# A linear-attention kernel feeding a two-layer perceptron: an earlier slot plan, half of the first q as float32, kv in two banks, and 12 idle matmuls ahead of the first turn of x

## The chip, the cores and the metric

The kernel runs on one core of one Trainium2 chip. The metric is the device time of one execution in microseconds (us). Before the change three runs gave 328.69, 330.32 and 331.72 us; the median is 330.32 us. TensorE (PE) does the matrix products and some transposes, VectorE (DVE) and ScalarE (ACT) the elementwise work, GpSimd (POOL) issues the loads that convert float32 to bfloat16, SyncE (SP) issues the stores and the transposing DMAs.

## The reference

Eight batches, eight heads, 576 positions, head size 64; model width 512, hidden width 2048.

```
kv  = einsum('bhsd,bhse->bhde', k, v)
out = einsum('bhsd,bhde->bhse', q, kv)
rms = sqrt(mean(out * out, axis=-1, keepdims=True) + 1e-06)
x   = (out / rms * g_norm)            # then laid out as (batch, position, 512)

mu, var = mean and variance of x over the 512
xn  = (x - mu) / sqrt(var + 1e-06) * g_ln
y   = x + maximum(xn @ w_ch1, 0.0) @ w_ch2
```

Inputs and the output are float32.

## The kernel before

**Tiling.** The 576 positions of a batch are spread over 128 partitions and four or five places each: partitions 0 to 63 hold five positions, partitions 64 to 127 hold four. A batch so has four full tiles of 128 positions and a remainder of 64; the remainders of two batches are put together into one tile ("rem", four of them).

**The steps of a batch b.** `load_batch` issues six DMAs on POOL (two each for k, v, q; they convert to bfloat16; `k_in`, `v_in`, `q_in` have two buffers, used by even and odd batches). `kv_of` does 40 small matmuls (L162) into one PSUM tile and copies the two diagonal halves into `kv_pack` (DVE L166, ACT L167). q has to be transposed: for batches 0 to 2 by PE (`q_turns`: DVE reorders q into `q_p`, L326; PE transposes, L140; ACT copies, L144), for the later ones by a transposing DMA (`turn_q_dma`: POOL reorders, L151; SP issues the DMA, L153). Per tile, `main_tile` does four matmuls (L179) and a chain (`tile_chain`): ACT square L182, DVE sum `ss` L184, ACT root L186, DVE reciprocal `inv` L188, then DVE `y` L190, `x_blk` L191, `stats` L193, their aggregate L194 and `xc` L196. `turn_x` transposes `xc`: on PE (L206, with an ACT copy L207) for batches 0 to 2, by a transposing DMA on SP (L209) for the others. `mm1` is the first layer (PE L268, ACT relu L271), `mm2` the second (PE L300, DVE sum `o_sb` L304, stores on SP).

**The order.** PE's order is written out by hand: it executes its instructions in the order in which the program issues them. The perceptron's matmuls are cut into slots, and `tick()` starts each slot: a slot of `mm2` is 4 matmuls of 512 columns, a slot of `mm1` is 4 of 512, 8 of 256 or 16 of 128. Batch 0 has slots 0 to 15 (first layer) and 16 to 31 (second), batch 1 has 32 to 47 and 48 to 63, batch 2 starts at 64, batch 3 at 96, and so on, 32 slots each; the remainder block is the last. An agenda says ahead of which slot kv, the turn of q, each tile and each turn of x of a later batch are put into PE's stream (`at`, the table `PLAN` and its defaults). The other engines are in-order as well, but their order is made by a planner from priorities (`due`); `keep_in_program_order` fixes the place of one instruction.

**Where the slots lie in the profile.** The first matmul of slot 0 starts at 27.05 us, that of slot 16 at 44.63, of slot 32 at 75.69; slot 64 begins with a tile at 120.49, slot 112 with a kv at 166.67. Ahead of slot 0 lie the start's loads, `q_turns(0)`, `kv_of(0)`, two tiles, and the turn of x of the first.

**Buffers that the text speaks of.** `qt_pool` holds three transposed q; one is given back when the remainder tile of its batch has been done. `ps_out` has two PSUM buffers, shared by the q transposes and the tiles. `outp` has four output tiles.

Of the kernel before, what the change touches and what calls it, by code (L numbers as in the profile page):

```python
# [2 lines left out]

# [11 lines left out]
def kernel(  # L15
# [11 lines left out]
    nc = tc.nc  # L27
# [51 lines left out]
    v_in = [consts.tile([128, H, JJ, D], bf16, name=f"v_in{i}") for i in range(NB)]  # L79
    kv_pack = [consts.tile([128, HP, 128], bf16, name=f"kv_pack{i}") for i in range(4)]  # L80

    def load(dst, t, b, h0=0, h1=H):
        nc.gpsimd.dma_start(dst[:64, h0:h1],
                            t[b, h0:h1, :S_LO, :].rearrange("h (p j) d -> p h j d", j=JJ))
        nc.gpsimd.dma_start(dst[64:, h0:h1, :J],  # L85
                            t[b, h0:h1, S_LO:, :].rearrange("h (p j) d -> p h j d", j=J))


    load(q_in[0], q, 0)
    nc.vector.memset(eps_sb, float(EPS))  # L90
    nc.scalar.activation(warm, eps_sb, func=AF.Sqrt)
    for i in range(NB):
# [50 lines left out]
                identity[:n, :n])  # L143
        nc.scalar.copy(q_t[:, j, :, :n], tp[:, :, :n])  # L144

    qts, held, blks, xcs = {}, {}, {}, {}

    def turn_q_dma(b):

        q_p = kv_in.tile([128, JJ, H, D], bf16, tag="qp", bufs=2)  # L150
        nc.gpsimd.tensor_copy(q_p.rearrange("p j h d -> p h j d"), q_in[b % NB])  # L151
        q_t = qt_pool.tile([128, JJ, HP, 128], bf16, tag="qt")
        nc.sync.dma_start_transpose(  # L153
            q_t.rearrange("p j hp t -> p (j hp) t"), q_p.rearrange("p j h d -> p (j h d)"))
        qts[b] = q_t

    def kv_of(b):
        kv_ps = ps_m.tile([128, HP, D], f32, tag="misc")
        for h in range(H):
            rows = slice(h % 2 * D, h % 2 * D + D)  # L160
            for j in range(JJ):
                nc.tensor.matmul(kv_ps[rows, h // 2, :], lhsT=k_in[b % NB][:, h, j, :],  # L162
                                 rhs=v_in[b % NB][:, h, j, :],
                                 start=(j == 0), stop=(j == JJ - 1))
        kvp = kv_pack[b % 4]
        nc.vector.tensor_copy(kvp[:D, :, :D], kv_ps[:D])  # L166
        nc.scalar.copy(kvp[D:, :, D:], kv_ps[D:])  # L167
        held[b] = kvp

    def tile_chain(mms, blk, ts, key):  # L170

        x_blk, mv_blk, xT_blk = blk
        x3 = x_blk[:, ts].rearrange("p (h d) -> p h d", h=H)
        x2 = x_blk[:, ts]
        o_ps = ps_out.tile([128, H, D], f32, tag="ops")
        o_flat = o_ps.rearrange("p h e -> p (h e)")
        for (rows, lhsT_of, kvp) in mms:
            for hp in range(HP):
                nc.tensor.matmul(o_flat[rows, hp * 128:(hp + 1) * 128],  # L179
                                 lhsT=lhsT_of(hp), rhs=kvp[:, hp, :], start=True, stop=True)  # L180
# [7 lines left out]
        nc.vector.reciprocal(inv, rms)  # L188
        y = work.tile([128, H, D], f32, tag="y")
        nc.vector.tensor_mul(y, o_ps, inv.to_broadcast([128, H, D]))  # L190
# [5 lines left out]
        nc.vector.scalar_tensor_tensor(xc, in0=x2, scalar=mv_blk[:, ts, 0:1], in1=g_ln_sb,  # L196
                                       op0=ALU.subtract, op1=ALU.mult)
        xcs[key] = xc

    def turn_x(blk, ts, key, on_pe):  # L200
        xc = xcs.pop(key)
# [120 lines left out]

    def q_turns(b):
        q_p = kv_in.tile([128, JJ, H, D], bf16, tag="qp", bufs=2)
        tc.keep_in_program_order(
            nc.vector.tensor_copy(q_p.rearrange("p j h d -> p h j d"), q_in[b % NB]))  # L326
# [8 lines left out]
    for j in (0, 1):  # L335
        due(-90 + 10 * j)
        main_tile(0, j)
    due(-90)
    turn_x(blks[0], 0, (0, 0), True)
    due(-70)  # L340
    main_tile(0, 2)


    PLAN = {1: dict(kv=23, q=23, tiles=[24, 26, 28, 30], turns=[32, 36, 40, 40], rem=48), 3: dict(load=28)}
    S1 = {1: 32, 2: 64}
    for b in range(1, B):
        p = PLAN.get(b, {})
# [66 lines left out]
```

## Time and profile before

| what | value |
|---|---|
| median of three runs | 330.32 us (328.69 to 331.72) |
| the profiled execution's own time | 331.43 us |
| its span, first to last instruction | 329.7 us |
| mean granted TensorE clock | 0.971 |
| PE busy | 283.2 us (86% of the span) |
| DVE busy | 172.5 us (52%) |
| ACT busy | 134.8 us (41%) |
| POOL busy | 52.8 us (16%) |
| last matmul of the run ends | 325.06 us |

The profile is of one execution. Busy time is the time in which an engine has at least one instruction running. Matmuls overlap each other, so PE can be busy all the time at quite different rates. "Granted clock" (PEclk) is the share of full TensorE clock that the chip's throttle gave. Idle time is written in square brackets behind an instruction, with what ended it.

### The profile page before, as it was taken

The page shows a single profiled execution, that of the slowest core. Times are in us where ns is not written, and L with a number is a line of the kernel's source. Part 1 is how long each engine was busy: PE and PEld are TensorE (multiplying, and loading weights), DVE is VectorE, ACT ScalarE, POOL GpSimd, SP SyncE. Part 2 cuts the span into 40 slices and gives each one's busy share as a digit, 9 for nine tenths or more (in the row PEclk, how much of TensorE's full clock was granted, in tenths as well). Part 3 has the DMA queues.
Part 4 walks back from the last instruction along what each step waited for, and adds up shares of the span by engine and source line. Part 5 has one row for each costly group of instructions (what it writes and reads, how often), then busy time and mean ns, then how long its engine had stood idle before and what let it go on. Part 6 is the DMA issues. An engine that isn't in the chain of part 4 may idle for free.

```text
span 329.7 us, 5123 instructions
## 1 busy us (share of the span) xinstructions
PE 283.2 (86%) x2032; PEld 154.3 (47%) x2060; DVE 172.5 (52%) x322; ACT 134.8 (41%) x265; POOL 52.8 (16%) x69
## 2 busy tenths in 40 slices
PE   0328997598792899997999999999999999999994
PEld 0318964347671444543444444445444444444441
DVE  3167403859764898199728745981884260010011
ACT  1325733246671237423731761274257116305500
POOL 7533405071421410302030000000000000000000
PEclk9999998969997899999999999999999999999998
DMA  7999999969829972499368401830331131031022
GB/s 100 199 206 203 201 201 174 200 89 223 109 48 169 167 132 51 65 203 166 80 91 150 97 18 37 171 65 18 80 80 34 32 87 25 2 84 43 2 64 64
DMA packets 61687, 34.84 MB, mean 106 GB/s; under 512 B 28256, under 2 KB 56928, under 8 KB 61664
## 3 DMA queue, kind: packets, MB, share of 16 engines
q0 software_dynamic: 29600, 18.35, 39.5%
q1 hardware_dynamic: 32064, 16.16, 24.0%
q8 instruction: 16, 0.26, 0.3%
q14 instruction: 7, 0.06, 0.1%
HBM read 37.00 MB, written 9.44 MB: 141 GB/s over the span
## 4 chain that ended last, share of the span: by engine, by line
PE 74%; DVE 10%; DMA 6%; ACT 4%; issue 3%; POOL 1%; POOLq 0%; DVEq 0%; SPq 0%; ACTq 0%
PE p L268 35%; PE p L300 34%; DMA v_in<-in_v_dram 3%; DMA q_t<-q_p 3%; DVE xc L196 2%; PE o_ps L179 2%; PE kv_ps L162 2%; DVE x_blk L191 1%; DVE ss L184 1%; DVE y L190 1%; DVE o_sb L304 1%; ACT xT_blk L207 1%; DVE stats L193 1%; ACT qt L144 1%; ACT m L271 1%
## 5 line engine op out<-in xcount | busy, mean ns | idle before, releaser
L268 PE MATMUL p<-xT_blk,w_sb 128*128 128x512 bf16 (+2 forms) x887 | 130.7, 306 | 4.6 <-ACT xT_blk L207 2.3
L300 PE MATMUL p<-w_sb,m 128*128 128x512 bf16 x557 | 131.8, 388 | 1.6 <-issue 0.8
L271 ACT ACTIVATE m<-p 128x512 bf16<-128x512 f32 x144 | 84.1, 594 | 43.9 <-PE p L268 42.9
L268 PEld LDWEIGHTS <-w_sb 128*128 128x128 bf16 x896 | 73.4, 100 | 56.2 <-issue 5.2
L300 PEld LDWEIGHTS <-m 128*128 128x128 bf16 x576 | 55.9, 100 | 64.3 <-issue 3.9
L304 DVE SCALAR_TENSOR_TENSOR o_sb<-p,rstd,x_blk 128x512 f32<-128x512 f32 x36 | 26.9, 746 | 91.6 <-PE p L300 79.6
L182 ACT ACTIVATE sq<-o_ps 128x512 f32<-128x512 f32 x36 | 21.4, 596 | 61.4 <-PE o_ps L179 61.1
L184 DVE TENSOR_REDUCE ss<-sq 128x8 f32<-128x512 f32 x36 | 24.3, 679 | 17.1 <-ACT sq L182 17.1
L196 DVE SCALAR_TENSOR_TENSOR xc<-x_blk,mv_blk,g_ln_sb 128x512 bf16<-128x512 f32 x36 | 32.8, 911 | 0.9
L190 DVE TENSOR_TENSOR y<-o_ps,inv 128x512 f32<-128x512 f32 x36 | 24.8, 690 | 3.2 <-PE o_ps L179 0.5
L193 DVE BATCH_NORM_STATS2 stats<-x_blk 128x6 f32<-128x512 f32 x36 | 24.9, 690 | 0.8
L191 DVE TENSOR_TENSOR x_blk<-y,g_norm_sb 128x512 f32<-128x512 f32 x36 | 24.7, 687 | 0.8
L140 PE MATMUL tp<-identity,q_p 128*128 128x128 bf16 (+1 forms) x60 | 6.7, 268 | 18.0 <-DVE q_p L326 16.4
L186 ACT ACTIVATE rms<-ss,eps_sb 128x8 f32<-128x8 f32 x36 | 10.8, 301 | 24.9 <-DVE ss L184 24.5
L151 POOL COPY q_p<-q_in 128x2560 bf16<-128x2560 bf16 x5 | 11.6, 2325 | 36.1 <-DMA q_t<-q_p 22.5
L85 POOL DMA_DIRECT2D k_in<-in_k_dram x8 | 6.0, 753 | 56.0 <-PE kv_ps L162 55.7
L166 DVE CAST kv_pack<-kv_ps 64x256 bf16<-64x256 f32 x8 | 3.3, 411 | 21.5 <-PE kv_ps L162 21.4
L140 PEld LDWEIGHTS <-q_p 128*128 128x128 bf16 (+1 forms) x60 | 5.1, 123 | 19.7 <-DVE q_p L326 17.0
L179 PE MATMUL o_ps<-kv_pack,q_t 128*128 128x128 bf16 (+1 forms) x100 | 9.2, 224 | 5.9 <-DMA q_t<-q_p 5.8
L206 PE MATMUL tp<-identity,xc 128*128 128x128 bf16 x48 | 5.1, 234 | 9.4 <-DVE xc L196 7.8
L144 ACT COPY qt<-tp 128x512 bf16<-128x512 bf16 (+1 forms) x15 | 7.5, 545 | 13.6 <-PE tp L140 13.6
L179 PEld LDWEIGHTS <-q_t 128*128 128x128 bf16 (+1 forms) x100 | 7.0, 101 | 11.6 <-DMA q_t<-q_p 6.3
(32 smaller groups left out, 101.6 us busy)
## 6 DMA issues: line engine op xcount, KB each, us to landing
out_dram<-o_sb SPq DMA_DIRECT2D x72, 128.0 KB, 2.3
w_sb<-in_moe_w_ch_dram POOLq DMA_DIRECT2D x8, 512.0 KB, 13.3
q_in<-in_q_dram POOLq DMA_DIRECT2D x8, 320.0 KB, 9.4
k_in<-in_k_dram POOLq DMA_DIRECT2D x8, 320.0 KB, 7.9
v_in<-in_v_dram POOLq DMA_DIRECT2D x7, 320.0 KB, 7.9
q_in<-in_q_dram POOLq DMA_DIRECT2D x8, 256.0 KB, 8.9
k_in<-in_k_dram POOLq DMA_DIRECT2D x8, 256.0 KB, 6.8
v_in<-in_v_dram POOLq DMA_DIRECT2D x7, 256.0 KB, 9.5
```

Source lines behind the costliest of these rows:

```text
L140: nc.tensor.transpose(tp[:, hp, :n], q_p[:n, j, 2 * hp:2 * hp + 2, :].rearrange("p h d -> p (h d)"), identity[:n, :n])
L179: nc.tensor.matmul(o_flat[rows, hp * 128:(hp + 1) * 128], lhsT=lhsT_of(hp), rhs=kvp[:, hp, :], start=True, stop=True)
L182: nc.scalar.activation(sq, o_ps, func=AF.Square)
L184: nc.vector.tensor_reduce(ss, sq, axis=AX.X, op=ALU.add)
L190: nc.vector.tensor_mul(y, o_ps, inv.to_broadcast([128, H, D]))
L191: nc.vector.tensor_mul(x3, y, g_norm_sb.to_broadcast([128, H, D]))
L193: nc.vector.bn_stats(stats, x2)
L196: nc.vector.scalar_tensor_tensor(xc, in0=x2, scalar=mv_blk[:, ts, 0:1], in1=g_ln_sb, op0=ALU.subtract, op1=ALU.mult)
L268: nc.tensor.matmul(p1[:, i, :], lhsT=w1_sb[:, kk, de * 128:(de + 1) * 128], rhs=blk[2][:, kk, sl], start=(kk == 0), stop=(kk == nK - 1))
L271: nc.scalar.activation(m1[:, de0:de0 + per, sl], p1, func=AF.Relu)
L300: nc.tensor.matmul(p2s[ts], lhsT=m1[:, de, ts * 128:(ts + 1) * 128], rhs=w2_sb[:, de, :], start=(de == 0), stop=(de == nDe - 1))
L304: nc.vector.scalar_tensor_tensor(o_sb, in0=p2s[ts], scalar=rstds.pop((b, ts))[:, ts], in1=blks[b][0][:, ts], op0=ALU.mult, op1=ALU.add)
```

## The change

- The upper half of the first q (partitions 64 to 127) is loaded as float32 by SP, ahead of the two small constants, into a buffer of `m1pool`; DVE converts it in `q_turns(0)`. The lower half is still loaded by POOL. POOL so issues seven loads ahead of the first weights instead of eight.
- `kv_of(0)` writes odd and even heads into two PSUM banks and works in two parts (four heads each); each part is copied into `kv_pack` when it is done.
- For batch 0, the part of a tile's chain from `y` on (now `tile_x`) is queued on DVE behind the `xc` of the tile before.
- 12 matmuls of 512 columns, whose result nobody reads, are put into PE's stream after the first two tiles and ahead of the first turn of x.
- The DMA turn of q (batches 3 to 7) reorders q on DVE in program order instead of on POOL; `qt_pool` has four buffers.
- The plan: batch 1's kv goes from slot 23 to 13, its q from 23 to 16, its tiles from 24, 26, 28, 30 to 17, 20, 24, 29, its turns of x from 32, 36, 40, 40 to 26, 31, 37, 40; the first remainder tile from 48 to 58. Batch 2's kv goes from 26 to 40, q from 27 to 41, tiles from 32, 38, 44, 50 to 42, 46, 51, 55, turns from 41, 47, 53, 59 to 51, 56, 60, 63. Batch 3: load from 28 to 17, kv from 48 to 56, q from 36 to 54, tiles from 52, 58, 64, 70 to 62, 67, 72, 77. The load of batch 4 goes from 40 to 42, of batch 5 from 72 to 58.
- The first layer of batch 1 takes its first two tiles together (256 columns instead of 128).

```
-    qt_pool = ctx.enter_context(tc.tile_pool(name="qt_pool", bufs=3))
+    qt_pool = ctx.enter_context(tc.tile_pool(name="qt_pool", bufs=4))
...
+    q_f = m1pool.tile([128, H, J, D], f32, tag="m1")
...
-    load(q_in[0], q, 0)
+    nc.sync.dma_start(q_f[64:], q[0, :, S_LO:, :].rearrange("h (p j) d -> p h j d", j=J))
+    nc.gpsimd.dma_start(q_in[0][:64], q[0, :, :S_LO, :].rearrange("h (p j) d -> p h j d", j=JJ))
...
     def turn_q_dma(b):
         q_p = kv_in.tile([128, JJ, H, D], bf16, tag="qp", bufs=2)
-        nc.gpsimd.tensor_copy(q_p.rearrange("p j h d -> p h j d"), q_in[b % NB])
+        tc.keep_in_program_order(
+            nc.vector.tensor_copy(q_p.rearrange("p j h d -> p h j d"), q_in[b % NB]))
...
     def kv_of(b):
         kv_ps = ps_m.tile([128, HP, D], f32, tag="misc")
-        for h in range(H):
-            rows = slice(h % 2 * D, h % 2 * D + D)
-            for j in range(JJ):
-                nc.tensor.matmul(kv_ps[rows, h // 2, :], lhsT=k_in[b % NB][:, h, j, :],
-                                 rhs=v_in[b % NB][:, h, j, :],
-                                 start=(j == 0), stop=(j == JJ - 1))
+        odd = ps2.tile([128, HP, D], f32, tag="p2", name="odd") if b == 0 else kv_ps
         kvp = kv_pack[b % 4]
-        nc.vector.tensor_copy(kvp[:D, :, :D], kv_ps[:D])
-        nc.scalar.copy(kvp[D:, :, D:], kv_ps[D:])
+        n = 2 if b == 0 else 1
+        for part in range(n):
+            for h in range(part * H // n, (part + 1) * H // n):
+                rows = slice(h % 2 * D, h % 2 * D + D)
+                for j in range(JJ):
+                    nc.tensor.matmul((odd if h % 2 else kv_ps)[rows, h // 2, :],
+                                     lhsT=k_in[b % NB][:, h, j, :], rhs=v_in[b % NB][:, h, j, :],
+                                     start=(j == 0), stop=(j == JJ - 1))
+            hps = slice(part * HP // n, (part + 1) * HP // n)
+            nc.vector.tensor_copy(kvp[:D, hps, :D], kv_ps[:D, hps])
+            nc.scalar.copy(kvp[D:, hps, D:], odd[D:, hps])
         held[b] = kvp
...
         nc.vector.reciprocal(inv, rms)
+        after = last_xc.get(chain) if chain is not None else None
+        with tc.issue_after(after) if after is not None else nullcontext():
+            last = tile_x(o_ps, inv, x_blk, mv_blk, ts, key)
+        if chain is not None:
+            last_xc[chain] = last.ins
...
-        tile_chain([(slice(0, 128), lambda hp: q_t[:, j, hp, :], kvp)], blks[b], j, (b, j))
+        tile_chain([(slice(0, 128), lambda hp: q_t[:, j, hp, :], kvp)], blks[b], j, (b, j),
+                   0 if b in (0,) else None)
...
     def q_turns(b):
         q_p = kv_in.tile([128, JJ, H, D], bf16, tag="qp", bufs=2)
-        tc.keep_in_program_order(
-            nc.vector.tensor_copy(q_p.rearrange("p j h d -> p h j d"), q_in[b % NB]))
+        if b == 0:
+            nc.vector.tensor_copy(q_p[64:, :J].rearrange("p j h d -> p h j d"), q_f[64:])
+            nc.vector.tensor_copy(q_p[:64].rearrange("p j h d -> p h j d"), q_in[0][:64])
+        else:
+            tc.keep_in_program_order(
+                nc.vector.tensor_copy(q_p.rearrange("p j h d -> p h j d"), q_in[b % NB]))
...
     for j in (0, 1):
         due(-90 + 10 * j)
         main_tile(0, j)
+
+    for n in (12,):
+        p1 = ps1.tile([128, 512], f32, tag="p1", name="p1")
+        for i in range(n):
+            nc.tensor.matmul(p1, lhsT=identity, rhs=qts[0][:, 0].rearrange("p a b -> p (a b)"),
+                             start=True, stop=True)
+        del p1
     due(-90)
     turn_x(blks[0], 0, (0, 0), True)
...
-    PLAN = {1: dict(kv=23, q=23, tiles=[24, 26, 28, 30], turns=[32, 36, 40, 40], rem=48), 3: dict(load=28)}
+    PLAN = {1: dict(kv=13, q=16, tiles=[17, 20, 24, 29], turns=[26, 31, 37, 40], rem=58),
+            2: dict(kv=40, q=41, tiles=[42, 46, 51, 55], turns=[51, 56, 60, 63]),
+            3: dict(load=17, kv=56, q=54, tiles=[62, 67, 72, 77]), 4: dict(load=42), 5: dict(load=58)}
...
-    mm1(1, 0, 1)
-    mm1(1, 1, 1)
+    mm1(1, 0, 2)
     mm1(1, 2, 2)
```

More of the change, by code (lines that the diff above doesn't have):

```diff
@@ L2 @@
 import logging
-from contextlib import ExitStack
+from contextlib import ExitStack, nullcontext
 import concourse.bass as bass
@@ L158, in kv_of, with tile_chain @@
         kv_ps = ps_m.tile([128, HP, D], f32, tag="misc")
-        for h in range(H):
-            rows = slice(h % 2 * D, h % 2 * D + D)
-            for j in range(JJ):
-                nc.tensor.matmul(kv_ps[rows, h // 2, :], lhsT=k_in[b % NB][:, h, j, :],
-                                 rhs=v_in[b % NB][:, h, j, :],
-                                 start=(j == 0), stop=(j == JJ - 1))
-        kvp = kv_pack[b % 4]
-        nc.vector.tensor_copy(kvp[:D, :, :D], kv_ps[:D])
-        nc.scalar.copy(kvp[D:, :, D:], kv_ps[D:])
+        odd = ps2.tile([128, HP, D], f32, tag="p2", name="odd") if b == 0 else kv_ps
+        kvp = kv_pack[b % 4]
+        n = 2 if b == 0 else 1
[9 more added lines that the diff above has]
+            nc.scalar.copy(kvp[D:, hps, D:], odd[D:, hps])
         held[b] = kvp
-    def tile_chain(mms, blk, ts, key):
+    def tile_chain(mms, blk, ts, key, chain=None):
         x_blk, mv_blk, xT_blk = blk
-        x3 = x_blk[:, ts].rearrange("p (h d) -> p h d", h=H)
-        x2 = x_blk[:, ts]
         o_ps = ps_out.tile([128, H, D], f32, tag="ops")
@@ L188, in tile_chain, with tile_x @@
         nc.vector.reciprocal(inv, rms)
+        after = last_xc.get(chain) if chain is not None else None
[3 more added lines that the diff above has]
+            last_xc[chain] = last.ins
+    def tile_x(o_ps, inv, x_blk, mv_blk, ts, key):
+        x3 = x_blk[:, ts].rearrange("p (h d) -> p h d", h=H)
+        x2 = x_blk[:, ts]
         y = work.tile([128, H, D], f32, tag="y")
@@ L195, in tile_chain @@
         xc = work.tile([128, Dm], bf16, tag="xc", bufs=4)
-        nc.vector.scalar_tensor_tensor(xc, in0=x2, scalar=mv_blk[:, ts, 0:1], in1=g_ln_sb,
+        last = nc.vector.scalar_tensor_tensor(xc, in0=x2, scalar=mv_blk[:, ts, 0:1], in1=g_ln_sb,
                                        op0=ALU.subtract, op1=ALU.mult)
         xcs[key] = xc
+        return last
     def turn_x(blk, ts, key, on_pe):
```

2 lines of the change are left out of this document (1 added, 1 removed).

## The prediction

> **What bounds the kernel now.** I read the run by stages first, cut at the slots that the code names: up to slot 0, slots 0 to 15, 16 to 31, 32 to 63, and (the last row) from slot 112 on. The columns are the stage, then busy us and instruction counts of each engine, granted clock, DMA share and rate.
>
> ```profile
> core 0: us, PE busy (x) PEld busy (x) DVE busy (x) ACT busy (x) POOL busy (x), PEclk, DMA share, GB/s
> 0.00:27.05 27.05, 6.13 (x76) 5.02 (x77) 10.95 (x29) 7.25 (x16) 14.06 (x25) 1.00 1.12 172
> 27.05:44.63 17.58, 17.49 (x273) 17.18 (x273) 7.95 (x16) 12.07 (x24) 6.29 (x9) 1.00 1.33 202
> 44.63:75.69 31.06, 24.12 (x205) 13.29 (x207) 15.78 (x29) 10.53 (x23) 11.66 (x14) 0.84 1.13 165
> 75.69:120.49 44.80, 34.10 (x350) 23.93 (x352) 33.64 (x62) 19.45 (x40) 12.98 (x12) 0.92 0.94 136
> ...
> 166.67:329.70 163.03, 157.26 (x872) 73.99 (x888) 71.07 (x129) 61.40 (x116) 2.74 (x4) 0.99 0.30 62
> ```
>
> The last stage is PE from end to end; it stays as it is. Before it PE idles 20.9 us in slot 0 and earlier, 6.9 in slots 16 to 31, 10.7 in slots 32 to 63, and in those two stages the clock is granted at 0.84 and 0.92. That is where the change works. Next, who PE waited for between 27 and 167 us (us in total, times, longest), and the three stretches of low clock:
>
> ```profile
> PE o_ps L179 <- DMA q_t<-q_p: 5.8, 1, 5.8
> PE tp L140 <- DVE q_p L326: 4.7, 2, 3.5
> PE p L268 <- ACT xT_blk L207: 2.3, 4, 0.9
> PE p L268 <- ACT m L271: 1.8, 1, 1.8
> PE tp L206 <- ACT xT_blk L207: 1.6, 1, 1.6
> PE tp L206 <- DVE xc L196: 1.5, 1, 1.5
> PE tp L140 <- ACT qt L144: 1.1, 4, 0.5
> ...
> 54.90:58.90 4.00, 3.67 (x17) 0.59 1.24 156
> 65.50:71.90 6.40, 5.97 (x31) 0.50 0.49 65
> 102.80:109.80 7.00, 3.93 (x17) 0.53 1.33 185
> ```
>
> These waits add up to 18.8 us. In the three stretches PE was busy 3.67, 5.97 and 3.93 us at a clock of 0.59, 0.50 and 0.53; at full clock this work takes 0.41, 0.50 and 0.47 of that less: 1.5 + 3.0 + 1.8 = 6.3 us.
>
> **The start.** From the timeline of the start and the chain of waits (start, us, what), with one undisturbed tile (93.82, 96.22) and one cold group of 512 columns (106.27):
>
> ```profile
> 16.65 0.82 PE L162 MATMUL kv_ps<-v_in,k_in 128*64 128x64 bf16 x20 [0.56 <-DMA v_in<-in_v_dram]
> 17.51 0.42 DVE L166 CAST kv_pack<-kv_ps 64x256 bf16<-64x256 f32 x1 [5.88 <-PE kv_ps L162]
> 17.96 0.37 ACT L167 CAST kv_pack<-kv_ps 64x256 bf16<-64x256 f32 x1 [2.96 <-DVE kv_pack L166]
> 18.38 1.01 PE L179 MATMUL o_ps<-kv_pack,qt 128*128 128x128 bf16 x8 [0.91 <-ACT kv_pack L167]
> 21.12 0.69 DVE L190 TENSOR_TENSOR y<-o_ps,inv 128x512 f32<-128x512 f32 x1
> 24.98 0.73 DVE L196 SCALAR_TENSOR_TENSOR xc<-x_blk,mv_blk,g_ln_sb 128x512 bf16<-128x512 f32 x1
> 25.77 0.61 PE L206 MATMUL tp<-identity,xc 128*128 128x128 bf16 x4 [6.38 <-DVE xc L196]
> ...
> 93.82 0.69 DVE L190 TENSOR_TENSOR y<-o_ps,inv 128x512 f32<-128x512 f32 x1
> 96.22 0.75 DVE L196 SCALAR_TENSOR_TENSOR xc<-x_blk,mv_blk,g_ln_sb 128x512 bf16<-128x512 f32 x1
> ...
> 106.27 1.91 PE L300 MATMUL p<-w_sb,m 128*128 128x512 bf16 x4
> 107.98 0.63 PE L206 MATMUL tp<-identity,xc 128*128 128x128 bf16 x4
> ...
> 27.05 4.67 PE p L268 x48
> 33.06 2.69 PE p L268 x48
> 27.06 0.68 POOL L85 DMA_DIRECT2D q_in<-in_q_dram  x1 [1.82 <-DMA w_sb<-in_moe_w_ch_dram]
> ```
>
> *kv copies.* DVE and ACT run one after the other, 0.91 us from kv to the tiles. With two banks they run side by side, each with half the columns: about 0.35. Saves 0.55 (0.2 to 0.6).
>
> *Chain.* From `y` to `xc` of the first tile pass 3.86 us, because DVE weaves the second tile in; undisturbed they take 2.40. Queueing the second tile behind saves 1.46 (1.0 to 1.5). The second tile's `xc` comes later for it, some 3 us behind the first; its turn stands at slot 3, behind 2.7 us of matmuls and the turn and copy, so this is hidden.
>
> *q as float32.* What ends the wait for kv is v's second half (16.65). POOL's queue carries one DMA fewer, but the other path carries twice the bytes of it, starting while the engines are not yet full. At the 200 GB/s of the second stage's row the 256 KB taken off POOL's queue are worth 1.3 us, and the 512 KB of float32 cost 2.6. I take 0.3 saved, between 1.3 saved (all of the float32 fits into the early gap) and 1.3 lost (none does). The conversion on DVE, 2,048 columns per partition, lies in and ahead of DVE's wait of 5.88 before 17.51; nothing else is queued there.
>
> *Idle matmuls.* Four cold ones of 512 columns take 1.71 us (106.27 to 107.98), 12 take 5.1. The gap that holds them is the 6.38 us ahead of the first turn, less the 1.46 of the chain: 4.9. So they cost 0.2 if they are cold to the last, nothing if the clock rises under them: 0.1. What they buy: slots 0 to 2 take 4.67 us (48 matmuls), the same work at 33.06 takes 2.69. The granted clock is shown as 1.00 there, but the spacing, 97 ns against 56, says that the array ran cold. At most 2.0 is won; the gap of some 1.3 us at the first turn and its copy remains cold ground, so I take 1.5 (0 to 2.0).
>
> *First weights.* Slot 3 needs the last quarter of the first weights, landed by 27.06 (POOL's issue was released by it). Slot 3 would come at 27.05 - 2.2 + 2.7 = 27.5. That is 0.4 of cover; 0.2 lost (0 to 1.0).
>
> Start together: -0.55 - 1.46 - 0.3 + 0.1 - 1.5 + 0.2 = **-3.5 us**.
>
> **The new plan.** Rows on loads, the q turn, POOL's copy, and the prices of a slot:
>
> ```profile
> 38.16 0.68 POOL L85 DMA_DIRECT2D v_in<-in_v_dram  x1 [0.72 <-DMA v_in<-in_v_dram]
> 51.76 1.20 POOL L85 DMA_DIRECT2D k_in<-in_k_dram  x1 [10.00 <-PE kv_ps L162]
> 51.87 0.81 DVE L326 COPY q_p<-q_in 128x2560 bf16<-128x2560 bf16 x1
> 55.57 1.48 PE L300 MATMUL p<-w_sb,m 128*128 128x512 bf16 x3 [0.34 <-issue]
> ...
> 113.02 2.32 POOL L151 COPY q_p<-q_in 128x2560 bf16<-128x2560 bf16 x1 [4.72 <-DMA q_t<-q_p]
> 113.03 2.85 DVE L196 SCALAR_TENSOR_TENSOR xc<-x_blk,mv_blk,g_ln_sb 128x512 bf16<-128x512 f32 x1
> ...
> 95.73 10.10 DMA q_t<-q_p
> DMA to landing us min/median/max: 4.9/6.2/13.7
> 158.10 8.63 PE p L268 x40
> ```
>
> *kv of batch 1 at slot 13.* PE is in order: if v of batch 1 is late, the whole stream waits. Its second DMA had landed by 38.16. Slot 13 comes three slots (0.9 us each, 2.69 / 3) ahead of 44.63, at 41.9, less 3.5: 38.4. So 0.2 lost (0 to 2).
>
> *q turns.* The waits of 4.7 us came because DVE's copy of q stood right behind kv's copies and, the second time, in the middle of tile chains. Now batch 1's q comes three slots after its kv, with DVE empty: nothing left. Batch 2's comes one slot after: kv_pack 0.42 and the copy 0.81 against a slot of 0.86 leave some 0.8 with the handing over. The 1.1 of waiting for ACT's copies stays.
>
> *q by DMA, batch 3.* The 5.8 us at the first tile of batch 3 are a transposing DMA that started at 95.73, when a third buffer came free, and took 10.10 with loads beside it. With a fourth buffer it can start at slot 54, and the tile stands at slot 62: 8 slots of 0.86 (8.63 for 40 matmuls), tiles, turns, kv, the remainder: about 8.7 us, against 0.81 for the copy and 6.2 for a median DMA. It fits, unless the load of batch 5 (slot 58) presses on it as in the 10.10 row: 0.5 lost (0 to 5).
>
> *POOL's copy.* At 113 us a POOL copy and an `xc` start together; `xc`, 0.73 to 0.75 elsewhere, takes 2.85 and ends just behind the copy. This stall made the turn wait 1.5 and pulled ACT's `xT` and relu with it (1.6, 1.8 of the list). On DVE the copy costs 0.81, and this cause is gone. The Trainium skill, SBUF — State Buffer, section "Who interferes with whom", says why: a DVE instruction with two SBUF inputs and a GpSimd one that reads SBUF exclude each other for the whole instruction. By its other half, that a DVE copy with both ports blocks GpSimd's writing of DMA descriptors, the change makes a new conflict: the issue at 51.76, beside DVE's copy, took 1.20 instead of 0.68. In the sum this is nothing, since from slot 54 on a load issued 0.5 us later is never the one waited for; at the start it is inside the 1.3 that v may lose.
>
> *Turns of x.* Of the 2.3 us, 0.7 stay: the last turn of batch 1 still stands right at slot 40. The last turn of batch 2 stands at slot 63, and between slots 42 and 63 (about 20.8 us) DVE has four tiles of 3.9 us (2.40 from `y` to `xc`, 0.75 for `xc`, and `ss` and `inv` ahead, taken like one `y`), three `o_sb` priced like `xc`, the copy and kv_pack: 19 us, and some 1.2 until it can start. That just fits; any disorder shows: 0.7 lost (0 to 2).
>
> Of the 18.8 us of waits 16.2 go (5.8, 3.9, 1.6, 1.8, 1.6, 1.5), 0.2 + 0.5 + 0.7 come.
>
> *Clock.* The first two cold stretches come with the two q turns, each with a wait ahead of it (some 4 us from the end of kv, which released the issue at 51.76, to 55.57, with nothing but transposes); the third follows the 5.8 us. Without waits a turn alone is 2.9 us (52.68 to 55.57). I keep one stretch like the first, 1.5 (0 to 6.3): **-4.8**.
>
> Slots of 256 columns cost as much as those of 128: 2,048 columns each.
>
> **Sum.** -3.5 + 0.2 - 16.2 + 0.5 + 0.7 - 4.8 = -23.1. From the profiled execution's 331.43 that is 308.3; it lies 1.1 above the median of the runs, so **307 us** (304 to 311 for this case alone).
>
> **Rivals.**
> *Clean* (0.20): no new wait, no cold stretch, the whole of the warm start: another 0.2 + 0.5 + 0.7 + 0.8 + 1.5 and about 1.5 at the start, 302. For it: DMA and DVE both have room on average.
> *Half clean* (0.22): each q turn throttles, the DMA turn of batch 3 takes 10 us again, DVE is late at slot 63: up to 4.8 + 4.5 + 1.3 more, 311 to 318. For it: two of two q turns were followed by a low clock. The Trainium skill, TensorE: Matmul & The Clock Gate, Part 4, says that transposes do not count as busy work in the way matmuls do; by that rule a turn is a hole in the activity even when PE does not wait. No run here separates the two.
> *The waits only move* (0.04): DVE, 33.64 busy of 44.80 already, becomes the bound between slots 17 and 63, and PE waits as long elsewhere. Then only start and clock are won: 331.43 - 3.3 - 4.8 - 1.1 = 322; if the clock falls too, 327.
> *Slower* (0.04): the clock. If the turns of x, q turns and short waits now packed into slots 16 to 63 keep the array at half rate throughout, each of the 48 slots costs 0.86 more: 41 us against 23 won, 348. It decides from 27 cold slots on. Against it: the three stretches hold only 17.4 us (4.0 + 6.4 + 7.0), beside waits that the change takes away.
>
> **Numbers.** 0.50 for 307, and the rivals as given. The range, 300 to 317, holds the forecast, nearly all of the clean and the half-clean case. A measurement of this kernel can tell about 1% (327.0 to 333.6) from no change. Faster by more: 0.50 + 0.20 + 0.22 + half of the moved waits, 0.94; same 0.02; slower 0.04.
>
> **What would show it.** Slot 0 at about 24.8 us, its first 48 matmuls in under 3.2 us; kv of batch 1 waiting under 1 us for v; slot 32 near 60, slot 64 near 97; no `xc` over 1 us; at most one cold stretch. I am wrong if PE waits for loads at slot 13 or 16 for several us, if the clock falls at every turn, or if DVE is late at slots 40 and 63.

## The result, and the profile after

The changed kernel took 319.13 us (three runs, 318.42 to 319.43) against 330.32. The ratio is 0.9659, 95% interval 0.9584 to 0.9735: faster by 3.4%. The forecast was 307, with a range up to 317: the direction was right, but the kernel won 11.2 us where 23.3 were expected, and 319.13 lies outside the range. In a second set of runs on another chip it took 320.21 us beside 330.64, ratio 0.972 (0.966 to 0.9781). The profiled execution took 318.42 us, with a span of 316.6 and a mean granted clock of 0.991. One execution below, e3's profiled one, was a disturbed one (346.73 us at a mean clock of 0.86) and is left out of e3's time.

The same stages as in the prediction, cut at slots 0, 16, 32, 64 and 112 of the changed kernel (stage, length, then busy us and counts of PE, PEld, DVE, ACT, POOL, granted clock, DMA share, GB/s):

```profile
24.32:42.64 18.32, 16.79 (x313) 16.07 (x312) 10.31 (x23) 10.57 (x23) 6.81 (x10) 1.00 1.32 203
42.64:62.79 20.15, 16.81 (x107) 8.85 (x110) 13.61 (x28) 9.00 (x19) 4.30 (x7) 1.00 1.36 211
62.79:105.97 43.18, 35.78 (x343) 24.71 (x345) 26.67 (x51) 20.99 (x43) 8.69 (x12) 0.96 0.86 130
...
153.18:316.60 163.42, 157.52 (x871) 73.97 (x888) 72.54 (x131) 61.08 (x116) 2.73 (x4) 0.99 0.36 69
```

Slot 0 begins 2.7 us earlier than before (27.05). Slots 16 to 31 shrank from 31.06 to 20.15 us: 10.9 of the 13.1 us between the two spans. Not all of that is work saved, because the plan also moved work out of this stage (kv of batch 1 to slot 13, kv and q of batch 2 to 40 and 41), and PE's matmuls in it fell from 205 to 107. Slots 32 to 63 only went from 44.80 to 43.18, and slot 64, for which the prediction has about 97, stands at 105.97. The last stage is what it was. So the question is what happened between slots 16 and 64. PE's waits, longest first (us in total, times, longest):

```profile
PE tp L144 <- DVE q_p L347: 10.9, 1, 10.9
PE o_ps L188 <- DMA q_t<-q_p: 6.5, 2, 4.5
PE tp L144 <- ACT qt L148: 3.4, 6, 2.2
PE kv_ps L173 <- DMA v_in<-in_v_dram: 2.7, 3, 1.1
PE kv_ps L173 <- ACT xT_blk L226: 1.6, 2, 0.9
...
PE p L320 <- DVE o_sb L324: 0.8, 1, 0.8
```

The first row is PE's wait for the first data, ahead of slot 0. The second is the wait that the change was to remove: 5.8 us before, 6.5 now, at two tiles in place of one. The third was 1.1 before. These are the two places where the prediction lost most.

**The transposing DMA of q.** From the timeline (start, us, engine, what, idle before it), around the DMA turn of batch 3:

```profile
88.17 0.78 DVE L156 COPY q_p<-q_in 128x2560 bf16<-128x2560 bf16 x1
89.24 0.68 POOL L86 DMA_DIRECT2D q_in<-in_q_dram  x1 [12.20 <-DVE q_p L156]
89.38 5.38 SPq L158 DMA_TRANSPOSE q_t<-q_p  x1
92.09 0.68 POOL L88 DMA_DIRECT2D k_in<-in_k_dram  x1 [1.47 <-PE kv_ps L173]
...
102.24 0.40 PE L188 MATMUL o_ps<-kv_pack,q_t 128*128 128x128 bf16 x4 [4.45 <-DMA q_t<-q_p]
```

and the two DMA turns in the chain of waits (start, us, what):

```profile
89.38 12.81 DMA q_t<-q_p
116.44 10.63 DMA q_t<-q_p
```

DVE's copy at 88.17 does two things when it ends. It makes `q_p` ready, so SP starts the transposing DMA (89.38). And it sets `q_in` free, for which POOL had waited 12.20 us: the load of batch 5's q starts 0.14 us earlier (89.24), and that of its k and v follows as soon as kv of batch 3 is done (92.09). The transposing DMA is in flight together with these loads (the last of them, v's, land only after it), takes 12.81 us, and the tile at slot 62 waits 4.45. Batch 4 is the same (10.63 us, and 2.01 of the 6.5 us of waits). These loads are 1.7 MB (three times 320 and 256 KB). After the first wait the clock is down, by the row of that stretch:

```profile
102.90:106.90 4.00, 3.78 (x14) 1.78 (x14) 2.21 (x5) 1.22 (x3) 0.00 (x0) 0.58 1.42 215
```

3.78 us of work at 0.58 lose 1.6 us.

**The q turn of batch 1.** The timeline around slot 16:

```profile
38.81 0.85 PE L173 MATMUL kv_ps<-v_in,k_in 128*64 128x64 bf16 x40 [0.97 <-DMA v_in<-in_v_dram]
...
41.75 0.83 DVE L350 COPY q_p<-q_in 128x2560 bf16<-128x2560 bf16 x1 [7.18 <-DMA q_in<-in_q_dram]
42.49 0.41 DVE L177 CAST kv_pack<-kv_ps 64x256 bf16<-64x256 f32 x1
42.94 0.37 ACT L178 CAST kv_pack<-kv_ps 64x256 bf16<-64x256 f32 x1 [4.47 <-DVE kv_pack L177]
43.33 1.57 ACT L291 ACTIVATE m<-p 128x512 bf16<-128x512 f32 x3
44.78 2.15 ACT L148 COPY qt<-tp 128x512 bf16<-128x512 bf16 x4
45.43 0.87 PE L144 MATMUL tp<-identity,q_p 128*128 128x128 bf16 x8 [2.18 <-ACT qt L148]
```

kv is done at 39.66, and DVE is idle, yet it copies `kv_pack` only at 42.49. The planner put the copy of q ahead of it in DVE's queue, and that one waits for q's load until 41.75: DVE stands still for 7.18 us, the last 2.1 of them with the copy of kv ready behind it. ACT's half of `kv_pack` waits in ACT's queue behind DVE's (4.47), three relus and the copies of the q turn wait behind that, and PE waits 2.18 in the middle of its turn.

**The start** went well. PE's timeline:

```profile
18.53 3.71 PE L366 MATMUL p<-qt,identity 128*128 128x512 bf16 x11 [0.22 <-issue]
23.25 0.40 PE L225 MATMUL tp<-identity,xc 128*128 128x128 bf16 x4 [1.01 <-DVE xc L214]
24.32 2.84 PE L288 MATMUL p<-xT_blk,w_sb 128*128 128x128 bf16 x48 [0.45 <-ACT xT_blk L226]
27.00 0.39 PE L225 MATMUL tp<-identity,xc 128*128 128x128 bf16 x4
```

The idle matmuls end a microsecond ahead of the first turn, and the first 48 matmuls pass in 2.68 us (24.32 to 27.00) where they took 4.67. Slot 0 is early in this execution also because v landed early: in c0, the same kernel on another chip, PE's last wait for v ends at 17.67 instead of 16.37, and slot 0 stands at 25.62.

### The profile page after: what moved, and what is told of

Read it like the earlier page. It is cut to its first block, busy times and chain, and to the rows that moved or that the text cites. A ratio compares the mean times of both kernels' runs of the same rounds, so it can differ in the third digit from the quotient of the medians.

```text
span 316.6 us, 5029 instructions
## 1 busy us (share of the span) xinstructions
PE 280.9 (89%) x1980; PEld 150.7 (48%) x2008; DVE 172.2 (54%) x329; ACT 133.6 (42%) x266; POOL 41.4 (13%) x63
## 4 chain that ended last, share of the span: by engine, by line
PE 54%; DMA 19%; DVE 16%; issue 4%; ACT 4%; POOL 0%; DVEq 0%; POOLq 0%; ACTq 0%
PE p L320 26%; PE p L288 25%; DMA q_t<-q_p 7%; DMA q_in<-in_q_dram 5%; DMA w_sb<-in_moe_w_ch_dram 4%; DMA k_in<-in_k_dram 3%; DVE x_blk L209 3%; DVE y L208 3%; DVE stats L211 2%; DVE ss L193 2%; DVE o_sb L324 2%; DVE xc L214 2%; PE o_ps L188 1%; PE kv_ps L173 1%; ACT m L291 1%
## 5 line engine op out<-in xcount | busy, mean ns | idle before, releaser
L288 PE MATMUL p<-xT_blk,w_sb 128*128 128x512 bf16 (+2 forms) x823 | 129.4, 313 | 1.9 <-ACT xT_blk L226 0.7
L320 PE MATMUL p<-w_sb,m 128*128 128x512 bf16 x558 | 129.3, 382 | 1.7 <-DVE o_sb L324 0.8
L288 PEld LDWEIGHTS <-w_sb 128*128 128x128 bf16 x832 | 70.4, 98 | 54.5 <-issue 3.1
L320 PEld LDWEIGHTS <-m 128*128 128x128 bf16 x576 | 55.0, 98 | 62.8 <-issue 1.6
L214 DVE SCALAR_TENSOR_TENSOR xc<-x_blk,mv_blk,g_ln_sb 128x512 bf16<-128x512 f32 x36 | 27.0, 750 | 1.1
L144 PE MATMUL tp<-identity,q_p 128*128 128x128 bf16 (+1 forms) x60 | 5.8, 239 | 15.0 <-DVE q_p L347 10.9
L177 DVE CAST kv_pack<-kv_ps 64x256 bf16<-64x256 f32 (+1 forms) x9 | 3.4, 379 | 22.9 <-PE kv_ps L173 22.9
L86 POOL DMA_DIRECT2D q_in<-in_q_dram x7 | 4.8, 687 | 59.9 <-DVE q_p L156 55.3
L144 PEld LDWEIGHTS <-q_p 128*128 128x128 bf16 (+1 forms) x60 | 4.4, 109 | 16.5 <-DVE q_p L347 10.9
L173 PE MATMUL kv_ps<-v_in,k_in 128*64 128x64 bf16 x300 | 7.5, 200 | 4.6 <-DMA v_in<-in_v_dram 2.7
L197 DVE RECIPROCAL inv<-rms 128x8 f32<-128x8 f32 x36 | 7.1, 198 | 7.7 <-ACT rms L195 7.7
## 6 DMA issues: line engine op xcount, KB each, us to landing
v_in<-in_v_dram POOLq DMA_DIRECT2D x7, 256.0 KB, 13.1
```

What stands on the lines that cost most here:

```text
L214: last = nc.vector.scalar_tensor_tensor(xc, in0=x2, scalar=mv_blk[:, ts, 0:1], in1=g_ln_sb, op0=ALU.subtract, op1=ALU.mult)
L288: nc.tensor.matmul(p1[:, i, :], lhsT=w1_sb[:, kk, de * 128:(de + 1) * 128], rhs=blk[2][:, kk, sl], start=(kk == 0), stop=(kk == nK - 1))
L320: nc.tensor.matmul(p2s[ts], lhsT=m1[:, de, ts * 128:(ts + 1) * 128], rhs=w2_sb[:, de, :], start=(de == 0), stop=(de == nDe - 1))
```

## The experiments

Kernels of one set ran on one chip and are compared with the kernel before on that chip: the first set (e1 to e4) with 330.28 us, the second (c0 to c3) with 330.64, the third (f0 to f3) with 330.43.

### e1: no idle matmuls

```
-    for n in (12,):
+    for n in ():
```

> The changed kernel without its 12 idle matmuls. Theory: they keep the array warm. Without them slots 0 to 2 (48 matmuls of 128 columns) take about 4.7 us again instead of the 2.7 of the changed kernel (24.32 to 27.00 us), and every slot behind comes later; the loads for kv at slot 13 wait 0.97 us in the changed kernel and take up part of this, so the end is 1 to 1.5 us later: 320 to 320.6. Rival: the 20 kv matmuls and 8 of the first tiles have already warmed the array; slots 0 to 2 stay under 3.2 us and the time within 0.5 us of 319.1.

318.58 us (316.63 to 319.91), ratio 0.9637 (0.9579 to 0.9695): no later than the changed kernel. But the reason is not that the array was warm without them: the first 48 matmuls took 3.80 us (25.71 to 29.51) in place of 2.68. What was lost there came back at slot 13, as the theory had it for a part. PE's timeline of e1, and of c0 (the changed kernel, with the idle matmuls), whose v landed as late as e1's (17.67 and 17.56):

```profile
39.99 0.85 PE L173 MATMUL kv_ps<-v_in,k_in 128*64 128x64 bf16 x40
```

```profile
40.14 0.85 PE L173 MATMUL kv_ps<-v_in,k_in 128*64 128x64 bf16 x40 [1.00 <-DMA v_in<-in_v_dram]
```

Without the idle matmuls kv of batch 1 does not wait for v; with them it waits 1.00 us and starts no earlier. In this kernel a good part of a faster start ends in that wait. f1, below, asks again with the wait gone.

### e2: the loads of batch b+2 wait until q of batch b has been turned

```
         qts[b] = q_t
+        guard = work.tile([128, 1], bf16, tag="guard", bufs=2)
+        guards[b] = nc.gpsimd.tensor_copy(guard, q_t[:, 0, 0, :1]).ins
...
+    def load_after(b):
+        g = guards.get(b - 2)
+        with tc.issue_after(g) if g is not None else nullcontext():
+            load_batch(b)
```

> The changed kernel, and the loads of batch b+2 (b = 3, 4, 5) are held on GpSimd behind a one-element copy out of the transposed q of batch b, so that they start only when the transposing DMA has landed. Theory: the transposing DMA of q is slow (12.8 us for batch 3, 10.6 for batch 4) because the load of q of batch b+2 overwrites the buffer that the same DVE copy has just read, so both start within 0.2 us of each other and share the DMA engines. Held back, it lands in 5 to 6.5 us; the waits of 4.45 us at slot 62 and 2.01 us at slot 84 go, and with the first the cold stretch behind it (1.8 us): 8 us less, 311. Rival: it is slow for what stands on its own queue (stores of 128 KB and transposes of x on SyncE); then it still takes over 10 us and the time stays within 1 us of 319.

312.68 us (309.9 to 313.37), ratio 0.9435 (0.9366 to 0.9504). The timeline of e2 shows the DMA alone, then the guard, then the loads:

```profile
92.49 3.26 SPq L164 DMA_TRANSPOSE q_t<-q_p  x1
97.58 0.26 POOL L167 COPY guard<-q_t 128x1 bf16<-128x1 bf16 x1 [17.43 <-DMA q_t<-q_p]
98.07 0.68 POOL L86 DMA_DIRECT2D k_in<-in_k_dram  x1 [0.23 <-issue]
100.73 0.39 PE L196 MATMUL o_ps<-kv_pack,q_t 128*128 128x128 bf16 x4
```

The row of the DMA view of e2 (issues, median us to landing):

```profile
q_t<-q_p SPq DMA_TRANSPOSE x5, 4.9
```

That is 6.5 us under the 319.13 of the changed kernel. The DMA lands in 4.9 us instead of 10.6 at the median, SP is busy with it for 3.26 us instead of 5.38, and the tile at slot 62 has no wait. Nothing else was changed, so the loads beside it are shown to be what made it late. Whether they do so by their bytes on the DMA engines or otherwise was not separated.

### e3: batch 1's and 2's copy of q behind the copy of kv on DVE

```
-            nc.vector.tensor_copy(kvp[:D, hps, :D], kv_ps[:D, hps])
+            kvc[b] = nc.vector.tensor_copy(kvp[:D, hps, :D], kv_ps[:D, hps]).ins
...
-            tc.keep_in_program_order(
-                nc.vector.tensor_copy(q_p.rearrange("p j h d -> p h j d"), q_in[b % NB]))
+            with tc.issue_after(kvc[b]):
+                tc.keep_in_program_order(
+                    nc.vector.tensor_copy(q_p.rearrange("p j h d -> p h j d"), q_in[b % NB]))
```

> The changed kernel, with the copy of q of batch 1 on VectorE queued behind the kv copy of batch 1 (the two are exchanged, nothing else). Theory: in the changed kernel VectorE waits 7.2 us for q's load at 41.75 us, the kv copy stands behind it, ScalarE's half of the kv copy behind that, and behind this three relus and the copies out of the q transposes: PE waits 2.18 us in the middle of the q turn. Exchanged, that wait falls under 0.5 us and slot 32 comes 2 us earlier; of this all that the wait for the transposing DMA of batch 3 (4.45 us) does not take back reaches the end: it starts 2 us earlier as well, so 317. Rival: the second tile's or the copies' buffers hold PE anyway; 318.5 to 319.5.

317.04 us (316.5 to 317.31, three executions), ratio 0.9589 (0.9536 to 0.9643), 2.1 us under the changed kernel's 319.13. c1 shows the same edit in a profile.

### e4: the start alone

All of the start's parts, with the old plan, the copies on GpSimd, three `qt` buffers and the old first layer.

> The parts of the change at the start alone (q upper half as float32, kv in two banks, the chain in order, 12 idle matmuls), with the plan, the GpSimd copies, the three buffers and the first layer of batch 1 of the kernel before. Theory: slot 0 at 24.3 us instead of 27.05 and slots 0 to 2 in 2.7 us instead of 4.7: 4.5 us earlier at slot 3, and nothing behind it is bound by loads: 325.5 to 326.5 (before: 330.3). Rival: the waits of the old plan (q turns of batches 1 and 2, the transposing DMA of batch 3) swallow it: 328 or more.

327.66 us (325.54 to 328.68, 10 runs), ratio 0.9907 (0.987 to 0.9943): 2.6 us, between the two expectations. Slot 16 comes at 41.62 us there, 3.0 earlier than in the trace of before, and 2.6 of it are there at the end.

### c0 and c1: the changed kernel again, and e2 and e3 together

> The changed kernel once more, as the reference point for the runs beside it on the same chip. 318 to 320; the transposing DMA of q of batch 3 takes over 10 us again, and PE waits 6 to 7 us for it at slots 62 and 84 together.

> The changed kernel with both cures: loads of batch b+2 held behind the transposed q of batch b, and the copy of q of batch 1 behind the kv copy. Theory: the two causes are separate, so their gains (6.4 and 2.1 us in the runs before) add up: 310 to 311. Rival: the 2 us won in the q turn of batch 1 only let PE wait longer for something behind it: 312 to 313.

c0 320.21 us (319.95 to 323.99), ratio 0.972 (0.966 to 0.9781); c1 309.16 (309.02 to 309.44), ratio 0.936 (0.9333 to 0.9388). The two mends give more than their sum: 11.1 us between c0 and c1 on one chip, where e2 and e3 stood 6.5 and 2.1 under the changed kernel's first median. c0's own median, 1.1 above that first one, is a part of the excess. Another part is the clock. c0's profile, of the slowest of its four executions (323.99), has a cold stretch behind the q turn of batch 1, which again waited 2.17 us for ACT:

```profile
46.00:54.00 8.00, 6.92 (x30) 3.46 (x31) 2.27 (x4) 3.42 (x8) 3.37 (x5) 0.57 1.40 198
```

6.92 us at 0.57 lose 3.0. e2's profile, which keeps the wait, has the same stretch at 0.58, those of e1 and c3 have it at 0.79. The execution shown above of the changed kernel had the same wait and 1.00 there, so the wait makes it possible and does not decide it. In c1 the turn looks like this in the timeline:

```profile
40.08 0.41 DVE L186 CAST kv_pack<-kv_ps 64x256 bf16<-64x256 f32 x1 [4.12 <-PE kv_ps L182]
42.34 0.83 DVE L360 COPY q_p<-q_in 128x2560 bf16<-128x2560 bf16 x1 [1.84 <-DMA q_in<-in_q_dram]
43.22 0.62 PE L149 MATMUL tp<-identity,q_p 128*128 128x128 bf16 x8 [0.40 <-DVE q_p L360]
```

and so in the stretch around it:

```profile
38.00:62.00 24.00, 21.95 (x217) 13.53 (x217) 14.94 (x29) 10.65 (x22) 6.50 (x10) 1.00 1.35 210
```

`kv_pack` is copied at once, q's load still ends at 42.3, and PE waits 0.40 for the copy and at most 0.45 for ACT within the turn. The mean clock of c1's four executions was 0.997 to 1.000; of e2's, which keeps the wait, 0.989, 0.989, 0.995 and 0.998, with times from 313.37 down to 309.9.

### c2 and f0: the plan moved by a slot

```
-    PLAN = {1: dict(kv=13, q=16, tiles=[17, 20, 24, 29], turns=[26, 31, 37, 40], rem=58),
+    PLAN = {1: dict(kv=14, q=17, tiles=[18, 21, 25, 29], turns=[26, 31, 36, 39], rem=58),
...
-            3: dict(load=17, kv=56, q=54, tiles=[62, 67, 72, 77]), 4: dict(load=42), 5: dict(load=58)}
+            3: dict(load=17, kv=57, q=54, tiles=[62, 67, 72, 77]), 4: dict(load=42), 5: dict(load=58)}
```

with e2's and e3's edits. f0 is the same kernel, on the third chip.

> As the run before, with the plan mended where PE waited in the trace of the changed kernel: kv, q and the first three tiles of batch 1 one slot later (kv waited 0.97 us for v at slot 13), its third and fourth turn of x at slots 36 and 39 (kv of batch 2 at slot 40 waited 0.94 us for ACT's copy of the turn at slot 40), and kv of batch 3 at slot 57 (0.67 us for the turn at 56). Theory: 1.5 to 2.5 us less than the run before, 308 to 309. Rival: these waits are handed on, no change.

> The fastest kernel so far (both cures and the mended plan) once more, as the point from which the parts of the start are taken away one at a time in the runs beside it. 307 to 308.

307.25 us (307.03 to 307.31), ratio 0.930 (0.9273 to 0.9328), and 307.06 (307.02 to 307.32), 0.9306 (0.9257 to 0.9355). c2 is 1.9 us less than c1 on the same chip: the kv of batches 2 and 3 no longer stand right behind a turn of x whose copy they wait for. These 1.6 us, in the list of PE's waits after the change and in c1's, are gone from c2's.

### c3: the copy of q for the DMA turns back on GpSimd

```
-        tc.keep_in_program_order(
-            nc.vector.tensor_copy(q_p.rearrange("p j h d -> p h j d"), q_in[b % NB]))
+        nc.gpsimd.tensor_copy(q_p.rearrange("p j h d -> p h j d"), q_in[b % NB])
```

on the changed kernel, and nothing else.

> The changed kernel with the copies of q of batches 3 to 7 on GpSimd again, as before the change; the rest as changed. Theory 1 (what I predicted): GpSimd's copies hold VectorE's xc for 2 us each; without the change of engine there are again xc of over 2 us, PE waits 1 to 2 us behind each that falls into slots 62 to 112, and the time is 2 to 4 us longer, 321 to 323. Theory 2: the harm of the changed kernel lies in pinning the copy at slot 54 on VectorE; GpSimd copies q of batch 3 at 76 to 80 us, as soon as it may, the DMA starts some 10 us earlier, and the wait of 4.5 us at slot 62 goes with its cold stretch: 6 us less, less the 2 to 4 of theory 1: 315 to 317.

313.02 us (312.88 to 314.11), ratio 0.9487 (0.945 to 0.9524): 7.2 us faster than c0 on the same chip, more than either expectation. c3's timeline, with the first tile of batch 3:

```profile
79.37 2.38 POOL L155 COPY q_p<-q_in 128x2560 bf16<-128x2560 bf16 x1
81.78 7.61 SPq L157 DMA_TRANSPOSE q_t<-q_p  x1
100.02 0.39 PE L187 MATMUL o_ps<-kv_pack,q_t 128*128 128x128 bf16 x4
```

From its views of the line that issues the DMA, and of `xc` (count, then ns at least, in the middle and at most):

```profile
DMA to landing us min/median/max: 4.9/11.1/16.8
```

```profile
L213 DVE SCALAR_TENSOR_TENSOR xc<-x_blk,mv_blk,g_ln_sb x36: 741/752/2568, 23.5 to 249.3; 128x512 bf16<-128x512 f32 x36
```

The transposing DMA is still slow (11.1 at the median). But GpSimd makes the copy as soon as its queue comes to it, right behind the loads of batch 4 (issued from 74.85 on): 8.8 us earlier than DVE, which had it fixed at slot 54 (88.17 in the changed kernel). So the DMA starts 18.2 us ahead of its tile (81.78, 100.02), and even the longest of the five, 16.8, would be in time. In the changed kernel it started 8.4 ahead of where the tile stands without its wait (89.38, 102.24 less 4.45). The stall of `xc` beside GpSimd's copy is back, up to 2.57 us, and costs PE little: 0.3 us in total in its list of waits for `xc`. The part of the change that took the copy from GpSimd and fixed it at slot 54 made the changed kernel slower, not faster; the two were not tried apart.

### f1, f2, f3: three parts of the start, undone one at a time on f0

f1 leaves out the idle matmuls as e1 does. f2 loads the whole first q by POOL, converted on the way, as before (DVE then reorders it in one copy):

```
-    nc.sync.dma_start(q_f[64:], q[0, :, S_LO:, :].rearrange("h (p j) d -> p h j d", j=J))
-    nc.gpsimd.dma_start(q_in[0][:64], q[0, :, :S_LO, :].rearrange("h (p j) d -> p h j d", j=JJ))
+    load(q_in[0], q, 0)
```

f3 gives up the order of the first tiles' chains on DVE:

```
-                   0 if b in (0,) else None)
+                   None)
```

> The run before this one without the 12 idle matmuls. In the changed kernel their loss cost nothing at the end (318.6 against 319.1), though slots 0 to 2 took 3.8 us instead of 2.7: theory, the wait for v of batch 1 at slot 13 took it up. Here kv stands a slot later and does not wait, so about 1 us must be lost: 308 to 308.5. Rival: the copy of q of batch 1, whose load lands at 42.6 us, is late enough to take it up again: within 0.3 us of the run beside it.

> The fastest kernel with the whole of the first q loaded and converted by GpSimd's queue, as before the change. My prediction took 0.3 us for the float32 load, between 1.3 won and 1.3 lost. Theory: v's second half lands within 0.5 us of the run beside it, because the float32 bytes share the same DMA engines: time within 0.5 us. Rival: GpSimd's queue carries 256 KB more ahead of v, which lands 1.3 us later, and the end with it: 308.3 to 309.

> The fastest kernel without the order on VectorE's chains of batch 0 (the second tile is woven into the first again). Theory: the first xc is 1.4 to 1.5 us later, slot 0 with it, and the end 1 to 1.5 us later: 308.3 to 309. Rival: the load of q of batch 1 is what sets the first slots: within 0.3 us.

f1 308.29 us (308.15 to 308.63), f2 306.25 (306.14 to 306.49), f3 309.58 (309.41 to 309.79), beside f0's 307.06. The first layer's 48 matmuls in PE's timelines, with the turns of x around them, for f0:

```profile
24.29 0.40 PE L234 MATMUL tp<-identity,xc 128*128 128x128 bf16 x4 [0.55 <-DVE xc L223]
25.36 2.84 PE L297 MATMUL p<-xT_blk,w_sb 128*128 128x128 bf16 x48 [0.45 <-ACT xT_blk L235]
28.04 0.39 PE L234 MATMUL tp<-identity,xc 128*128 128x128 bf16 x4
```

for f1:

```profile
25.69 4.31 PE L297 MATMUL p<-xT_blk,w_sb 128*128 128x128 bf16 x48 [0.25 <-ACT xT_blk L235]
29.83 0.39 PE L234 MATMUL tp<-identity,xc 128*128 128x128 bf16 x4
```

and for f3:

```profile
25.99 0.40 PE L234 MATMUL tp<-identity,xc 128*128 128x128 bf16 x4 [3.24 <-DVE xc L223]
27.06 4.47 PE L297 MATMUL p<-xT_blk,w_sb 128*128 128x128 bf16 x48 [0.45 <-ACT xT_blk L235]
31.37 0.39 PE L234 MATMUL tp<-identity,xc 128*128 128x128 bf16 x4
```

Without the idle matmuls (f1) the 48 take 4.14 us instead of 2.68, and 1.2 of it reach the end. Without the chain's order (f3) the first turn comes 1.7 us later, and the 48 take 4.31 though the idle matmuls ran: PE idled 3.24 us between them. So f3 loses 2.5 at the end, more than the chain alone.

In f2, v's second half is there earlier. PE's timeline of f0:

```profile
17.41 0.29 PE L182 MATMUL kv_ps<-v_in,k_in 128*64 128x64 bf16 x2 [0.81 <-DMA v_in<-in_v_dram]
```

and of f2:

```profile
16.70 0.29 PE L180 MATMUL kv_ps<-v_in,k_in 128*64 128x64 bf16 x2 [0.70 <-DMA v_in<-in_v_dram]
```

The float32 half delays v by 0.7 us, and costs 0.8 at the end. Neither expectation had this sign. f2 is the fastest kernel of all: 0.9281 (0.924 to 0.9321).

## Why the prediction was right or wrong

The sum gave 308.3 on the profiled execution's own time; the profiled execution of the changed kernel took 318.42, 10.1 more. Term by term, in us (plus is a loss):

| term of the sum | forecast | measured | difference |
|---|---|---|---|
| tiles waiting for the DMA turn of q | +0.5 | 4.45 + 2.01 | +6.0 |
| q turn of batch 1, beyond the 1.1 that stay | 0 | 3.4 - 1.1 | +2.3 |
| kv of batch 1 waiting for v | +0.2 | 0.97 | +0.8 |
| kv late at slots 40 and 56 (1.6), sum late at slot 24 (0.8) | +0.7 | 1.6 + 0.8 | +1.7 |
| cold stretches kept | 1.5 | 1.6 | +0.1 |
| slot 0 (27.05 before) | -2.2 | -2.7 | -0.5 |
| the first 48 matmuls, warm (4.67 before) | -1.5 | -2.0 | -0.5 |

These add up to 9.9. The row on slot 0 is of this one execution: c0's slot 0 stands 1.4 earlier than before, not 2.7.

**q by DMA, batch 3: the step that failed.** The failed term is the +0.5 for a DMA that "fits" between slots 54 and 62; it measured 6.5. The prediction had the failure in it as a condition, "unless the load of batch 5 presses on it as in the 10.10 row", and priced it 0.5. It should have asked what starts that load. The load takes over the buffer that the very same DVE copy reads. The end of the copy so releases both: the pressure was certain, not a chance. The DMA took 12.81 us against the 8.7 of cover, and e2 shows the cause. The row that warned of it stood in the prediction: the one DMA turn that PE had waited for took 10.10 beside loads, against 6.2 at the median.

**POOL's copy: wrong in its sign.** The prediction took the stalls of `xc` beside it as the cause of 1.5 + 1.6 + 1.8 us of waits and expected them to go with the copy. No `xc` took over a microsecond afterwards, as the prediction said, but c3 shows that with GpSimd's copy in the new plan PE waits only 0.3 us for `xc`, and that giving it up cost 7.2. What the move did besides changing the engine was to fix the copy's place in the order, and so the start of the DMA behind it. Of the moved step, the prediction counted the copy (0.81) and not the start of the DMA.

**q turns, "nothing left": wrong.** The reason given, three slots between kv and q, holds on PE's order alone. On DVE the planner had exchanged the two copies: DVE stood for 7.18 us at the one that waits for a load, and the copy of kv, ready at 39.66, came at 42.49, with ACT's work behind it. e3 gave 2.1 us back, and c1's profile shows the turn as the prediction had it. The order on DVE could not be read in the trace of before; the prediction should have bounded it with the 3.5 us wait of the same kind in its own list.

**Clock: right in size, in part by luck.** One cold stretch was kept at 1.5, and 1.6 was measured, but not where it was meant: it was to be one like the first, which came with a q turn, and it came behind the DMA wait that was to go. That no q turn was followed by one held in this execution; c0's had one of 3.0 there.

**Idle matmuls and chain: right.** "At most 2.0 is won, I take 1.5": the 48 matmuls went from 4.67 to 2.68, and f1 puts the part that reaches the end at 1.2. The chain took 2.40 from `y` (20.04) to `xc` (22.44), as forecast; f3 puts what it saves at 1.7 at the first turn. From the end of PE's last wait for v to slot 0 pass 7.95 us in the changed kernel, in c0 and in f2, and 10.40 before: 2.45 saved, where kv's copies and the chain, less 0.1, were to save 1.9.

**q as float32: wrong in sign, inside its bounds.** 0.3 saved was taken, between 1.3 saved and 1.3 lost; f2 against f0 shows 0.8 lost. In the profile after, PE's wait for v ended 0.3 earlier than in the one before (16.37 against 16.65) just as forecast, but that is luck of the execution: in the profiles of all eleven runs with the float32 half (e1 to e4, c0 to c3, f0, f1, f3) it ended between 17.38 and 17.76, and without it, in f2, at 16.70.

**kv at slot 13: a term mis-sized.** It waited 0.97 where 0.2 was taken. The 0.2 supposed that v had landed by 38.16 as before; it landed at 38.8, and in c0, where slot 0 came 1.3 later, at 40.1, so that kv waited 1.00 all the same. Why it lands later is open.

**Waits that go: right for the most part.** The waits of 4.7 us for DVE's copies are 0.5 in all, and the 1.8 us for relu are 0.5. The turn at slot 63, "just fits", did not wait, nor in c1 and c2, where no DMA wait stands ahead of it. With the two failed steps mended and nothing else, c1 took 309.16, inside the 304 to 311 of the prediction's own case.

Of the rivals, *half clean* had one part right (the DMA turn of batch 3 takes 10 us again) and the nearest time, 311 to 318; its two others, a low clock at each q turn and DVE late at slot 63, did not come in this execution. That the change itself would slow the DMA, and do it at two batches, no case had.

## What to carry to other kernels

When a step is moved to another engine or another place, ask what its end releases: here one copy set a DMA going and at the same moment gave the loads a free buffer, and the two got in each other's way; a wait put in front of the loads was worth 6.5 us. In an in-order queue an instruction that waits for a load goes behind everything that is already able to run, and where a planner orders the queue this has to be written down. A faster start or a filled gap is only worth what the next wait behind it leaves over, so it is measured again after that wait is gone.

## What the runs showed of the hardware

- A transposing DMA of 128 x 2560 bf16 landed in 4.9 us at the median of e2, where the loads wait for it (6.7 at most), and in 10.4 to 12.8 beside loads of up to 1.7 MB in the two profiles of the changed kernel; in c3 one took 16.8. SP was busy issuing it for 3.1 to 3.3 us in e2 and 5.3 to 5.4 beside the loads of the changed kernel.
- Twelve idle matmuls warmed the array for the real ones (the 48 of the first layer in 2.68 us with them, f0, and 4.14 without, f1); a gap of 3.24 us behind them undid it (f3), one of about a microsecond did not (the changed kernel, 22.24 to 23.25). The Trainium skill, TensorE: Matmul & The Clock Gate, section "Why this matters for your kernels", puts the limit at gaps of about 3 us, and these runs agree. The granted clock does not always show it. The stretch of the 48 matmuls in f1, at the slow pace:

```profile
25.69:29.95 4.26, 4.26 (x51) 4.26 (x51) 4.06 (x9) 2.13 (x5) 1.00 (x2) 1.00 1.24 208
```

and in f3, at the slow pace too:

```profile
27.06:31.46 4.40, 4.40 (x50) 4.40 (x50) 3.31 (x7) 2.10 (x5) 1.44 (x2) 0.61 1.27 205
```

- A q turn of batch 1 with waits of 0.45 us at most was followed by full clock in all six profiles that have it (38 to 62 us in c1, c2 and f0 to f3: 1.00). With a wait of 2.2 in it, a low clock followed in four of five (c0 0.57, e2 0.58, e1 and c3 0.79 in 46 to 54 us) and none in the first profile of the changed kernel. So the turn alone did not lower the clock here; whether transposes by themselves keep the array warm stays open.
- A GpSimd DMA issue beside a DVE copy took longer again, here at the start of the changed kernel (timeline), 1.43 us against 0.68 of the POOL issues above:

```profile
5.94 1.49 DVE L346 CAST q_p<-q_f 64x2048 bf16<-64x2048 f32 x1 [2.13 <-DMA q_f<-in_q_dram]
6.32 1.43 POOL L123 DMA_DIRECT2D w_sb<-in_moe_w_ch_dram  x1
```

This agrees with the rule of the Trainium skill that the prediction names (SBUF — State Buffer, "Who interferes with whom"). It fell on a load of weights, not on v. That v came 0.7 us later with the float32 load is measured; whether by its bytes on the DMA engines or otherwise was not separated.
- Not tried: an earlier place for DVE's copy of batch 3, GpSimd's copy together with the guard, the new plan without the start's parts, and f2's form without the guard.
